# Chunk attention and two expert layers: the attention probabilities transposed on VectorE and exchanged by GpSimd's DMAs

## The chip, the cores and the metric

One core of one Trainium2 chip runs the kernel. The metric is the device time of one execution in microseconds; lower is better. The engines named below are TensorE (PE, with its weight loads PEld), VectorE (DVE), ScalarE (ACT), GpSimd (POOL) and SyncE (SP, which issues DMAs).

## The reference, cut to what matters

Attention runs within chunks of 64 tokens, 8 batches of 8 heads, 576 tokens each, 64 numbers per head. Its result is the input of two dense layers over 4608 tokens.

```python
def _attn_ref(q, k, v):                      # chunks of 64 tokens
    scores = scale * np.matmul(q_c, k_c.transpose(0, 1, 2, 4, 3))
    scores = scores - np.max(scores, axis=-1, keepdims=True)
    attn = np.exp(scores)
    attn = attn / (np.sum(attn, axis=-1, keepdims=True) + 1e-09)
    return np.matmul(attn, v_c)

def _moe_ref(x, w_in, w_out):                # 512 -> 2048 -> 512
    h = x @ w_in
    return (h * np.cos(h)) @ w_out

def _moe2_ref(x, w_in, w_out, g_ln):         # 512 -> 1024 -> 512
    h = x @ w_in
    solu = h * softmax(h)
    return (layernorm(solu) * g_ln) @ w_out
```

## The kernel before, in words

The 4608 tokens are worked through in nine blocks `j` of 512. The first expert layer is a list of 144 steps (`steps`, line 79), one for each block and each of the 16 columns of 128 hidden units. Step `n` runs `mm_in(n)` (12 matmuls of 128x512 into `h`, lines 570 to 572), on VectorE and ScalarE the cosine of steps `n` and `n - 1` (`act_h`, `dve_r`, `act_sin`, `dve_g`, `split_g`: tiles `hs`, `kt`, `r`, `gh`, `gl`), and `mm_out(n - 2)` (12 matmuls into `y`, lines 637 to 639). Every float32 product is made of three matmuls of split halves (`xh`, `xl` with `whi`, `wlo`). The second expert layer follows the first, with its first segments beside the first layer's last steps.

Attention is cut into 20 units. The first four (two chunks each) run before the steps. The others hold four chunks of all 8 heads, so that two units make one block of 512 tokens. Units 4 and 5 (`i < NAT`) load q and k in another order and are spread over four steps each (`tight`). Units 6 to 19, fourteen of them, are spread over eight steps each by the list `wide` (lines 819 to 824): each entry names a step counted from the unit's first, a place in that step (`early` is after `mm_in`, `mid` before `mm_out`, `late` after it) and a piece. `place` (lines 835 to 846) gives the unit's first step; for a unit of block `j` it is 17 or 9 steps ahead of the block's own first step.

The pieces of a wide unit are `att_tr` (q and k transposed in 32x32 blocks on VectorE, line 427, tiles `qt` and `kt`), `att_qk` (64 matmuls of 64x64 on TensorE, tile `sc`), `att_max`, `att_sub`, `att_exp`, `att_sum`, `att_mul` (softmax, tile `p`), `att_pt` (8 full 128x128 transposes of `p` on TensorE into PSUM, tile `pt`, line 503), `att_ptc` (one copy of 128x1024 on ScalarE from PSUM, tile `ptb`, line 508), `att_pv` (64 matmuls of 64x64 against the values, tile `x`) and `att_x` (split of the result into `xh` on ScalarE and `xl` on VectorE). `load_next` loads q and k of the next unit in 32 DMAs of 32 KB on SyncE, `load_next_v` its values in 4 of 128 KB. `sc`, `pt` and `x` follow each other in the one buffer of `ps_a` (tag `a`, two PSUM banks). `qt`, `kt`, `p` and `ptb` follow each other in the two SBUF buffers of tag `t` (`work`, line 315). `qi`, `ki` and `vi` have one buffer each.

The order of an engine's instructions is made by the framework's scheduler: it takes what is ready in the order of the program, so that pieces may be moved ahead of their place. `tc.keep_in_program_order` pins an instruction behind the one that the program traced last on the same engine; `att_tr` is pinned so. Semaphore waits are put in by the framework. Many instructions are recorded under line 104, the helper's; there the tile names tell them apart.

In the second layer `blocks32` and `shuffle` (lines 954 to 978) transpose an activation: 32x32 blocks on VectorE (tile `bt`), then 16 DMAs per block of 512 tokens on SyncE that move each 32-partition group to its place (tile `lt`). Weights of the second layer are prepared during the first, in `prep_w2in` at steps 55 and 71 and `prep_w2out` at 87, 88, 103 and 104 (lines 1058 to 1068). GpSimd runs a few set-up instructions and, in the second layer, two small ones per tile (line 939, tile `rs`).

Of the kernel before, what the change touches and what calls it, by code (L numbers as in the profile page):

```python
# [29 lines left out]
def kernel(  # L30
# [12 lines left out]
    nc = tc.nc  # L43
# [5 lines left out]
    CH = 64  # L49
# [5 lines left out]
    NF = F1 // P  # L55
# [18 lines left out]
    NB = 8  # L74
# [81 lines left out]
    def wtile(dt, name, n=1024):  # L156
        return wp.tile([P, n], dt, tag="w", name=name)
# [141 lines left out]
    UNITS = [(2 * i, 2) for i in range(SUB)] + [(c, 4) for c in range(8, NT // CH, 4)]  # L299
    NU = len(UNITS)  # L300
    HU = H // 2


    NAT = SUB + 2
    GA = 8

    def small(i):
        return i < SUB

    def work(i, shape, tag, name):  # L310

        if small(i) or (i == SUB + 1 and tag != "t"):
            t = wtile(F32, name, 512 if small(i) else 1024)
        else:
            t = ap_.tile([P, 1024], F32, tag=tag, name=name, bufs=2 if tag == "t" else 1)
        letters = "abcde"[:len(shape)]
        sizes = {x: n for x, n in zip(letters, shape)}
        return t.rearrange(f"p ({' '.join(letters)}) -> p {' '.join(letters)}", **sizes)
# [17 lines left out]
    v0 = su.tile([P, HU, 2 * SUB, D], F32, name="v0")  # L336
# [86 lines left out]
    def att_tr(i, name):  # L423
        src, dst = (qi, qt) if name == "q" else (ki, kt)
        o = work(i, (H, 4, 32), "t", f"{name}t")
        tc.keep_in_program_order(
            nc.vector.transpose(out=o.rearrange("p h x t -> p x h t"), in_=src.pop(i))
        )
        dst[i] = o.rearrange("p h x t -> p h (x t)")
# [3 lines left out]
    def natural(i, ap):  # L433
        return ap.rearrange("p (a g) -> p g a", a=GA) if SUB <= i < NAT else ap
# [58 lines left out]
    pt, ptb = {}, {}  # L493

    def att_pt(i):
        p = pr.pop(i)
        x = UNITS[i][1] // 2 * HU
        if small(i):
            t = ps_h.tile([P, x, P], F32, tag="h", name="pt")
        else:  # L500
            t = ps_a.tile([P, x, P], F32, tag="a", name="pt")
        for y in range(x):
            pe.transpose(out=t[:, y], in_=p[:, y].rearrange("p r k -> p (r k)"), identity=ident)
        pt[i] = t
# [8 lines left out]
    def att_pv(i):  # L513
        n = UNITS[i][1]

        t = (ps_y if small(i) else ps_a).tile([P, 2, 512], F32, tag="y" if small(i) else "a", name="x")
        a, b = vi.pop(i, None), ptb.pop(i)
        for y in range(n * HU // 2):
            for row in range(2):
                for col in range(2):  # L520
                    rs = slice(row * CH, (row + 1) * CH)
                    if small(i):
                        w, c = divmod(y, n)
                        u = 2 * w + col
                        m, p = v0[rs, u, UNITS[i][0] + c], b[rs, u, c * CH:(c + 1) * CH]
                    else:
                        u, cc = divmod(y, 2)
                        m, p = a[rs, cc, 2 * u + col], b[rs, cc * HU + u, col * CH:(col + 1) * CH]
                    pe.matmul(
                        out=t[col * CH:(col + 1) * CH, row, y * CH:(y + 1) * CH],  # L530
                        lhsT=m,
                        rhs=natural(i, p),
                        start=True,
                        stop=True,
                    )
        xps[i] = t[:, :, 0:n * HU // 2 * CH]
# [172 lines left out]
    if True:  # L709
# [23 lines left out]
        for c in range(4):  # L733
            sync.dma_start(
                out=gcol[32 * c:32 * (c + 1)],
                in_=g_ln.rearrange("(c q p) -> c p q", c=4, p=32)[c],
# [20 lines left out]
        att_mul(0)  # L757
        tok(2)
        att_pt(0)
        att_max(1)  # L760
        att_sub(1)
# [7 lines left out]
        att_mul(1)  # L769
        tok(3)  # L770
        att_pt(1)
        att_max(2)
        att_sub(2)
# [5 lines left out]
        att_sum(2)  # L779
        att_mul(2)  # L780
        att_pv(0)
        att_pt(2)
        att_max(3)
        att_sub(3)
        att_exp(3)
        att_ptc(2)
        att_pv(1)
        att_pv(2)
        att_sum(3)
        att_mul(3)  # L790
# [24 lines left out]
        def load_next_v(i):  # L815
# [3 lines left out]
        wide = (  # L819
            (0, "early", lambda i: att_tr(i, "q")), (1, "early", lambda i: att_tr(i, "k")),  # L820
            (1, "late", att_qk), (1, "late", load_next), (2, "early", att_max), (3, "early", att_sub),
            (3, "mid", att_exp), (4, "early", att_sum), (5, "early", att_mul), (5, "late", att_pt),
            (6, "early", att_ptc), (6, "late", att_pv), (6, "late", load_next_v), (7, "early", att_x),
        )
        tight = (
            (0, "early", lambda i: att_nat(i, "q")), (0, "early", lambda i: att_natc(i, "q")),
# [8 lines left out]
        def place(i, n, pieces):  # L835
            for at, when, what in pieces:
                att.setdefault((n + at, when), []).append((what, i))

        for i in range(SUB, NU):
            j, o = divmod(UNITS[i][0] * CH, T)  # L840
            if j == 1:
                place(i, 0 if o == 0 else NB // 2, tight)
            elif j == 2:
                place(i, NF + (0 if o == 0 else NB - 1), wide)
            else:
                place(i, j * NF - NF - 1 if o == 0 else j * NF - NB - 1, wide)

        def run(n, when):
            for what, i in att.get((n, when), ()):
# [176 lines left out]
        for n in range(NSTEP + LAG + 1):  # L1026
# [20 lines left out]
            r = n - NB  # L1047
# [38 lines left out]
        for x in range(first_seg, 2 * (NI + LAG2) + 4):  # L1086
            i, seg = divmod(x, 4)
            segment(i, seg)
            t, half = 2 * i - LAG2 + seg // 2, seg % 2
# [34 lines left out]
```

## Time and profile before

| | us |
|---|---|
| median of 3 runs | 1317.0 |
| lowest, highest | 1316.44, 1317.3 |
| the profiled execution, device time | 1315.48 |
| its span on the core | 1313.7 |

The profile is of one execution. The page begins with the busy time of each engine; below it the span is cut into slices, and groups of instructions are listed by line, tile and shape. A row of a timeline gives the start, the duration, engine, line, the operation with output and input tiles, shapes and a count of merged instructions; in square brackets stands how long the engine had been idle before and what ended that. Matmuls are pipelined and overlap, so that the spacing of their starts, not their duration, tells what one costs. PEclk is the granted share of TensorE's full clock.

### The profile page before, as it was taken

What the parts mean: (1) busy time and instruction counts of PE and PEld (TensorE: products, weight loads), DVE (VectorE), ACT (ScalarE), POOL (GpSimd) and SP (SyncE); (2) the same over time, 40 slices, a digit from 0 to 9 for tenths busy, and PEclk for the clock granted to TensorE, in tenths of its full rate; (3) what the DMA queues carried; (4) which work ended last, traced back from release to release, by engine and by line L of the source; (5) the groups of instructions that cost most, each with busy time, mean ns of one, the idle gap of its engine ahead of it and who ended that gap; (6) DMA issues with size and microseconds to landing.
All of it is one profiled execution on the core that took longest, in us unless ns stands there. A gap on an engine that the chain in (4) does not pass through costs nothing.

```text
span 1313.7 us, 20245 instructions
## 1 busy us (share of the span) xinstructions
PE 1270.9 (97%) x7652; PEld 1016.4 (77%) x7652; DVE 977.1 (74%) x1608; ACT 789.3 (60%) x1143; POOL 30.7 (2%) x79
## 2 busy tenths in 40 slices
PE   5899999999999999999999999999989999999998
PEld 4566777888887787888887888888768888888886
DVE  4887988676779879878878866667786686766751
ACT  4877876666655656556556545537665655655552
POOL 0000000000000000000000000000110000000000
PEclk9899999999999999999999999999989999999999
DMA  9942344331344344353343410450464543445224
GB/s 243 212 108 82 111 132 92 90 77 30 58 135 135 63 133 133 65 124 97 78 108 97 95 27 1 150 215 28 154 190 114 149 131 99 122 111 145 64 63 107
DMA packets 240930, 143.44 MB, mean 109 GB/s; under 512 B 176832, under 2 KB 217280, under 8 KB 239296
## 3 DMA queue, kind: packets, MB, share of 16 engines
q1 hardware_dynamic: 240736, 142.02, 41.4%
q8 instruction: 60, 0.98, 0.3%
q14 instruction: 38, 0.31, 0.1%
q10 hardware_dynamic: 96, 0.13, 0.0%
HBM read 83.63 MB, written 39.58 MB: 94 GB/s over the span
## 4 chain that ended last, share of the span: by engine, by line
PE 76%; DVE 10%; ACT 5%; issue 4%; SPq 3%; DMA 2%; POOL 0%; ACTq 0%; DVEq 0%; POOLq 0%
PE h L570 8%; PE y L637 8%; PE y L638 7%; PE y L639 7%; PE h L572 7%; PE h L571 7%; PE o L994 5%; PE o L992 5%; PE o L993 5%; PE h L862 4%; PE h L864 3%; PE h L863 3%; SPq L104 3%; DVE z L104 2%; PE x L104 1%
## 5 line engine op out<-in xcount | busy, mean ns | idle before, releaser
L570 PE MATMUL h<-xh,whi 128*128 128x512 f32 x576 | 232.6, 404 | 1.6 <-ACT xh L104 1.3
L571 PE MATMUL h<-xl,whi 128*128 128x512 f32 x576 | 226.2, 393 | 0.9 <-DVE xl L104 0.9
L572 PE MATMUL h<-xh,wlo 128*128 128x512 f32 x576 | 226.2, 393 | 0.1
L637 PE MATMUL y<-gh,whi 128*128 128x512 f32 x544 | 213.0, 397 | 4.8 <-ACT gh L104 3.8
L638 PE MATMUL y<-gl,whi 128*128 128x512 f32 x544 | 215.3, 396 | 0.3 <-DVE gl L104 0.3
L639 PE MATMUL y<-gh,wlo 128*128 128x512 f32 x544 | 214.9, 395 | 0.0
L599 ACT ACTIVATE r<-r 128x512 f32<-128x512 f32 x144 | 90.8, 631 | 166.0 <-DVE r L593 165.7
L607 DVE SCALAR_TENSOR_TENSOR hs<-r,hs 128x512 f32<-128x512 f32 x136 | 93.7, 689 | 81.6 <-ACT r L600 81.2
L570 PEld LDWEIGHTS h<-xh,whi 128*128 128x128 f32 x576 | 108.8, 189 | 27.9 <-issue 1.6
L104 ACT ACTIVATE gh<-hs 128x512 fp32r<-128x512 f32 x136 | 85.5, 629 | 74.0 <-DVE hs L607 71.0
L571 PEld LDWEIGHTS h<-xl,whi 128*128 128x128 f32 x576 | 108.7, 189 | 25.0 <-issue 1.7
L572 PEld LDWEIGHTS h<-xh,wlo 128*128 128x128 f32 x576 | 108.6, 189 | 24.2 <-issue 0.5
L104 DVE TENSOR_TENSOR gl<-hs,gh 128x512 fp32r<-128x512 f32 x136 | 93.4, 687 | 44.8 <-ACT gh L104 44.6
L637 PEld LDWEIGHTS y<-gh,whi 128*128 128x128 f32 x544 | 101.4, 188 | 31.7 <-ACT gh L104 7.5
L638 PEld LDWEIGHTS y<-gl,whi 128*128 128x128 f32 x544 | 102.2, 188 | 26.2 <-DVE gl L104 2.3
L639 PEld LDWEIGHTS y<-gh,wlo 128*128 128x128 f32 x544 | 102.1, 188 | 23.6
L577 ACT ACTIVATE hs<-h 128x512 f32<-128x512 f32 x144 | 85.2, 592 | 56.7 <-PE h L572 46.2
L992 PE MATMUL o<-whi,lh 128*128 128x512 f32 x288 | 113.5, 394 | 1.6 <-ACT lh L104 1.6
L994 PE MATMUL o<-whi,ll 128*128 128x512 f32 x288 | 113.2, 393 | 0.7 <-DVE ll L104 0.5
L993 PE MATMUL o<-wlo,lh 128*128 128x512 f32 x288 | 113.3, 393 | 0.0
L590 DVE SCALAR_TENSOR_TENSOR r<-kt,hs 128x512 f32<-128x512 int32 x144 | 99.1, 688 | 16.4 <-ACT kt L585 13.9
L862 PE MATMUL h<-whi,yh 128*128 128x512 f32 x252 | 99.6, 395 | 9.9 <-DVE tp L890 9.9
(112 smaller groups left out, 2078.3 us busy)
## 6 DMA issues: line engine op xcount, KB each, us to landing
lt<-bt SPq DMA_DIRECT2D x144, 128.0 KB
yr<-yd SPq DMA_DIRECT2D x18, 896.0 KB
yd<-ts SPq DMA_DIRECT2D x18, 512.0 KB
out<-os SPq DMA_DIRECT2D x142, 64.0 KB
vi<-in_v SPq DMA_DIRECT2D x64, 128.0 KB
qi<-in_q SPq DMA_DIRECT2D x224, 32.0 KB
ki<-in_k SPq DMA_DIRECT2D x224, 32.0 KB
st<-in_moe_w_in SPq DMA_DIRECT2D x10, 512.0 KB
```

Of the source, the lines that this page charges most:

```text
L104: ins = getattr(self.engine, name)(*args, **kwargs)
L570: nc.tensor.matmul(out=t, lhsT=wa, rhs=xh[j][:, kk, :], start=(kk == 0), stop=False)
L571: nc.tensor.matmul(out=t, lhsT=wa, rhs=xl[j][:, kk, :], start=False, stop=False)
L572: nc.tensor.matmul(out=t, lhsT=wb, rhs=xh[j][:, kk, :], start=False, stop=(kk == KD - 1))
L590: nc.vector.scalar_tensor_tensor(out=r, in0=kt, scalar=-TWO_PI_HI, in1=h, op0=ALU.mult, op1=ALU.add)
L637: nc.tensor.matmul(out=o, lhsT=wa, rhs=a, start=head, stop=False)
L638: nc.tensor.matmul(out=o, lhsT=wa, rhs=b, start=False, stop=False)
L639: nc.tensor.matmul(out=o, lhsT=wb, rhs=a, start=False, stop=last)
L862: nc.tensor.matmul(out=ps, lhsT=a, rhs=whi, start=kk == 0, stop=False)
L992: nc.tensor.matmul(out=o, lhsT=hi, rhs=whi, start=(f == 0), stop=False)
L993: nc.tensor.matmul(out=o, lhsT=hi, rhs=wlo, start=False, stop=False)
L994: nc.tensor.matmul(out=o, lhsT=lo, rhs=whi, start=False, stop=(f == NF2 - 1))
```

## The change

For the units from `NAT` on, `att_pt` no longer transposes on TensorE. VectorE transposes `p` in 32x32 blocks into a new tile `t` of the same tag and size (named `ptr`), and 16 DMAs from GpSimd's queue, each of 32 partitions by 1 KB, move block row `c` of column group `g` to block row `g` of column group `c` in the tile `ptb`. The ScalarE copy `att_ptc` is gone for all wide units. `att_pv` reads the moved operand as two pieces of 32 instead of 64 contiguous numbers. In the list, `att_mul` goes from early in step 5 to late in step 4, the transpose from late in 5 to late in 4, `att_pv` from late in 6 to early in 8, `load_next_v` from late in 6 to late in 8 and `att_x` from early in 7 to early in 9. Each wide unit's first step is one earlier (the first unit's two). Units 0 to 5 keep the old way.

```diff
--- before.py
+++ after.py
@@ -495,6 +495,24 @@
     def att_pt(i):
         p = pr.pop(i)
         x = UNITS[i][1] // 2 * HU
+        if i >= NAT:
+
+            t = work(i, (4, x, 32), "t", "ptr")
+            o = work(i, (4, x, 32), "t", "ptb")
+            tc.keep_in_program_order(
+                nc.vector.transpose(
+                    out=t.rearrange("p g x s -> p x g s"),
+                    in_=p.rearrange("p x r (h s) -> p x (r h) s", s=32),
+                )
+            )
+            for g in range(4):
+                for c in range(4):
+                    nc.gpsimd.dma_start(
+                        out=o[32 * g:32 * (g + 1), c].rearrange("p x s -> p (x s)"),
+                        in_=t[32 * c:32 * (c + 1), g].rearrange("p x s -> p (x s)"),
+                    )
+            ptb[i] = o
+            return
         if small(i):
             t = ps_h.tile([P, x, P], F32, tag="h", name="pt")
         else:
@@ -522,14 +540,18 @@
                     if small(i):
                         w, c = divmod(y, n)
                         u = 2 * w + col
-                        m, p = v0[rs, u, UNITS[i][0] + c], b[rs, u, c * CH:(c + 1) * CH]
+                        m, p = v0[rs, u, UNITS[i][0] + c], natural(i, b[rs, u, c * CH:(c + 1) * CH])
                     else:
                         u, cc = divmod(y, 2)
-                        m, p = a[rs, cc, 2 * u + col], b[rs, cc * HU + u, col * CH:(col + 1) * CH]
+                        m, x = a[rs, cc, 2 * u + col], cc * HU + u
+                        if i < NAT:
+                            p = natural(i, b[rs, x, col * CH:(col + 1) * CH])
+                        else:
+                            p = b[rs, 2 * col:2 * col + 2, x, :]
                     pe.matmul(
                         out=t[col * CH:(col + 1) * CH, row, y * CH:(y + 1) * CH],
                         lhsT=m,
-                        rhs=natural(i, p),
+                        rhs=p,
                         start=True,
                         stop=True,
                     )
@@ -819,8 +841,8 @@
         wide = (
             (0, "early", lambda i: att_tr(i, "q")), (1, "early", lambda i: att_tr(i, "k")),
             (1, "late", att_qk), (1, "late", load_next), (2, "early", att_max), (3, "early", att_sub),
-            (3, "mid", att_exp), (4, "early", att_sum), (5, "early", att_mul), (5, "late", att_pt),
-            (6, "early", att_ptc), (6, "late", att_pv), (6, "late", load_next_v), (7, "early", att_x),
+            (3, "mid", att_exp), (4, "early", att_sum), (4, "late", att_mul), (4, "late", att_pt),
+            (8, "early", att_pv), (8, "late", load_next_v), (9, "early", att_x),
         )
         tight = (
             (0, "early", lambda i: att_nat(i, "q")), (0, "early", lambda i: att_natc(i, "q")),
@@ -841,9 +863,9 @@
             if j == 1:
                 place(i, 0 if o == 0 else NB // 2, tight)
             elif j == 2:
-                place(i, NF + (0 if o == 0 else NB - 1), wide)
+                place(i, NF - 2 if o == 0 else NF + NB - 2, wide)
             else:
-                place(i, j * NF - NF - 1 if o == 0 else j * NF - NB - 1, wide)
+                place(i, j * NF - NF - 2 if o == 0 else j * NF - NB - 2, wide)
 
         def run(n, when):
             for what, i in att.get((n, when), ()):
```

## Rows read from the trace of the kernel before

**Rows 1.** The page's engine table: busy us, share of the span, instructions.

```profile
PE 1270.9 (97%) x7652; PEld 1016.4 (77%) x7652; DVE 977.1 (74%) x1608; ACT 789.3 (60%) x1143; POOL 30.7 (2%) x79
```

**Rows 2.** Stretches: length, then busy us (instructions) by engine, granted clock, DMA share, GB/s.

```profile
core 0: us, PE busy (x) PEld busy (x) DVE busy (x) ACT busy (x) POOL busy (x), PEclk, DMA share, GB/s
160.00:830.00 670.00, 665.05 (x4563) 536.06 (x4562) 529.29 (x767) 403.06 (x601) 0.00 (x0) 1.00 0.36 87
490.00:660.00 170.00, 168.45 (x1152) 136.19 (x1151) 144.09 (x215) 101.22 (x149) 0.00 (x0) 1.00 0.43 102
```

**Rows 3.** TensorE's waits: who waited for whom, us in total, times, longest.

```profile
PE h L862 <- DVE tp L890: 9.9, 8, 6.0
```

**Rows 4.** Timeline of TensorE around one unit's transposes: start, us, instruction.

```profile
326.48 0.39 PE L639 MATMUL y<-gh,wlo 128*128 128x512 f32 x1
326.70 1.04 PE L104 MATMUL pt<-ident,p 128*128 128x128 f32 x8
...
327.81 0.39 PE L571 MATMUL h<-xl,whi 128*128 128x512 f32 x1
328.04 0.39 PE L572 MATMUL h<-xh,wlo 128*128 128x512 f32 x1
```

**Rows 5.** Groups of instructions by form: busy us, mean ns, idle before.

```profile
L607 DVE SCALAR_TENSOR_TENSOR hs<-r,hs 128x512 f32<-128x512 f32 x136 | 93.7, 689 | 81.6 <-ACT r L600 81.2
...
L587 DVE TENSOR_SCALAR kt<-hs 128x512 int32<-128x512 f32 x96 | 40.6, 423 | 11.3 <-ACT hs L577 9.9
...
L104 PE MATMUL pt<-ident,p 128*128 128x128 f32 x144 | 20.6, 285 | 2.4 <-DVE p L104 2.4
...
L427 DVE STREAM_TRANSPOSE qt<-qi 128x1024 f32<-128x1024 f32 x14 | 17.3, 1237 | 0.0
```

**Rows 6.** Timeline of an ordinary step, VectorE's and TensorE's.

```profile
325.26 0.69 DVE L104 TENSOR_TENSOR gl<-hs,gh 128x512 fp32r<-128x512 f32 x1 [0.89 <-ACT gh L104]
...
330.57 0.39 PE L638 MATMUL y<-gl,whi 128*128 128x512 f32 x1
```

**Rows 7.** GpSimd's line 939: duration ns min/median/max, first and last start us.

```profile
L939 POOL TENSOR_TENSOR rs<-va,nhalf x36: 547/548/1520, 901.4 to 1274.8; 128x1 f32<-128x1 f32 x36
```

**Rows 8.** Timeline of the last shuffle: VectorE's, SyncE's and ScalarE's.

```profile
1275.69 2.47 DVE L964 STREAM_TRANSPOSE bt<-h 128x1024 f32<-128x1024 f32 x2 [0.98 <-ACT h L945]
...
1279.10 10.06 SPq L974 DMA_DIRECT2D lt<-bt  x16
...
1291.16 1.06 ACT L104 ACTIVATE lh<-lt 128x1024 fp32r<-128x1024 f32 x1 [1.69 <-DMA lt<-bt]
```

**Rows 9.** Timeline of SyncE's queue: one unit's query loads, 32 KB each.

```profile
536.88 7.71 SPq L104 DMA_DIRECT2D qi<-in_q  x16
```

**Rows 10.** Timeline of VectorE in one ordinary unit, 534 to 583 us.

```profile
535.62 1.24 DVE L427 STREAM_TRANSPOSE qt<-qi 128x1024 f32<-128x1024 f32 x1
...
560.88 1.23 DVE L104 TENSOR_TENSOR p<-p,s 128x1024 f32<-128x1024 f32 x1
...
579.49 1.22 DVE L104 TENSOR_TENSOR xl<-x,xh 128x1024 fp32r<-128x1024 f32 x1 [0.22 <-ACT xh L104]
...
582.50 1.24 DVE L427 STREAM_TRANSPOSE qt<-qi 128x1024 f32<-128x1024 f32 x1
```

**Rows 11.** Timeline of TensorE in the same unit.

```profile
546.12 1.16 PE L104 MATMUL sc<-kt,qt 64*64 64x64 f32 x64
...
575.94 1.16 PE L104 MATMUL x<-ptb,vi 64*64 64x64 f32 x64
```

**Rows 12.** Timeline of a unit beside a weight preparation, VectorE's and TensorE's.

```profile
388.40 1.24 DVE L427 STREAM_TRANSPOSE qt<-qi 128x1024 f32<-128x1024 f32 x1
...
417.87 1.24 DVE L427 STREAM_TRANSPOSE kt<-ki 128x1024 f32<-128x1024 f32 x1
...
430.51 1.22 DVE L104 TENSOR_TENSOR p<-p,s 128x1024 f32<-128x1024 f32 x1
...
435.66 1.16 PE L104 MATMUL x<-ptb,vi 64*64 64x64 f32 x64
```

**Rows 13.** Busy time in a stretch beside that preparation, columns as in rows 2.

```profile
396.00:424.00 28.00, 27.09 (x177) 21.64 (x176) 26.77 (x43) 14.88 (x27) 0.00 (x0) 1.00 0.45 147
```

## What the change should do to the time

> **What bounds the kernel now.** I read the engine table of the page first, to see which engine is full: TensorE 1270.9 of 1313.7 us, VectorE three quarters, GpSimd 2% [rows 1]. A share is an average, so I then cut the span at the stages and read busy time by stretch. The fourteen units that the change touches lie almost wholly between 160 and 830 us. There TensorE is idle for 670 - 665.05 = 4.95 us, at a granted clock of 1.00 (the 2.4 GHz level), VectorE is busy 79% of the time (85% in the fullest stretch) and GpSimd not at all [rows 2]. So in this stage time is what TensorE is given to do, and an instruction taken from it is worth its whole place in the queue. Last I read TensorE's waits: the largest, 9.9 us on `tp`, belongs to the second expert layer, after this stage [rows 3].
>
> **What is removed.** Per unit, 8 transposes on TensorE and one copy on ScalarE. The mean of a transpose, 285 ns [rows 5], is not its price: matmuls overlap, and so I price the hole that the eight leave between their neighbours. From the last `y` matmul before them to the second `h` matmul after them is 327.81 - 326.48 = 1.33 us; two ordinary spacings of 0.23 us (327.81 to 328.04) would be 0.46. The eight cost 0.87 us [rows 4]. Fourteen units: 12.2 us. The copies run on ScalarE, which is at 60% [rows 1]; nothing but `x` on TensorE waits for them, so they bring nothing further.
>
> **What is added on VectorE.** One 32x32-block transpose of 128x1024 per unit. The kernel does the same form for q and k: 1237 ns [rows 5]. Fourteen make 17.3 us, on an engine with 15 to 21% free [rows 2]; priced at nothing, because the instructions behind it are early. In an ordinary step `gl` is written at 325.26 + 0.69 = 325.95 and first read by `y` L638 at 330.57, so VectorE may be 4.6 us late before TensorE notices [rows 6]. If that cover were gone, all of the 17.3 us would be paid.
>
> **What is added on GpSimd.** 16 DMAs of 32 KB per unit, 224 in all, SBUF to SBUF. Its queue holds nothing else in this stage: the first of its `rs` instructions starts at 901.4 us [rows 7]. No row shows a DMA issued from GpSimd, so I bound the exchange, from the end of VectorE's transpose to the last landing, by the nearest rows. The nearest is the kernel's own shuffle of `bt` into `lt`: 16 DMAs between the same partition groups, four times the bytes, from SyncE. At the end of the program it is bare: transposes end at 1278.16, the DMAs are issued from 1279.10 for 10.06 us (0.63 each), the last landing releases `lh` at 1291.16. That is 13.0 us = 16 x 0.63 + 2.9 around it [rows 8]. Cheaper: 32 KB loads on SyncE, 7.71 us for 16 (0.48 each), which gives 10.6 us [rows 9]. Dearer: the longest GpSimd instruction of that line, 1.52 us [rows 7], taken 16 times, gives 27.2 us. I take 0.8 us each, 16 us, nearer to the shuffle since the pattern is the same, but above it since the queue is another.
>
> The Trainium skill (DMA: Bandwidth & Descriptors, Latency and other measured facts) puts about 1 us on the first byte of a DMA from GpSimd and 0.6 on one from SyncE; if each of the 16 cost that 1 us, the exchange would be an estimated 18.9 us. No row here shows it.
>
> **Is there room for it?** An ordinary unit, in its own time: `qt` at 535.62, probabilities multiplied until 560.88 + 1.23 = 562.11, next unit's `qt` at 582.50, which is 8 steps later [rows 10]. Less the two attention blocks in it (1.16 us each as `sc` and `x` show, [rows 11]) and the transposes' 0.87, a step is about 5.5 us, half of it 12 matmuls of 0.23. The multiply keeps its place behind the same `r` (late in step 4 instead of early in step 5). The new transpose is pinned behind it alone and ends at 563.35. Two instructions then wait for the DMAs:
> - `x` on TensorE goes from late in step 6 to early in step 8: 575.94 [rows 11] + 3 x 2.75 - 0.87 = 583.3. Window: 583.3 - 563.35 = 19.95 us. A microsecond late here is a microsecond lost.
> - The next unit's `qt` on VectorE. The change puts five tiles per unit instead of four through the two buffers of tag `t`, so `qt` falls on the buffer that the DMAs read. At 582.50 - 0.87 = 581.6 its window is 18.3 us; behind it stand `hs` and `gl`, with 4.6 us of their own.
>
> So 16 us fits, and 13 us with ease. The break-even is (19.95 - 2.9) / 16 = 1.07 us per DMA.
>
> **What moves.** A unit starts one step earlier and has its `x` early in its step 8 instead of late in 6, so in the kernel's steps `x` comes half a step (2.75 us) later and its evacuation one step; for every second unit the next block's `mm_in` needs the result. From the start of `x` to the end of `xl` is 579.49 + 1.22 - 575.94 = 4.8 us [rows 10, 11]; after the change 1.16 + 2.75 + 5.5 = 9.4 us lie between: free. The value loads behind `x` on SyncE's queue start half a step later, for a use eight steps off: free. Query and key loads come one step earlier with their unit. TensorE's wait for 16 landings in place of one copy: `x` already waits for four `vi` DMAs and `sc` for none, yet both blocks take 1.16 us [rows 11]; nothing.
>
> **Where it is tight.** Beside the units that start at steps 55 and 71 a second-layer weight is prepared on VectorE. There `qt` is at 388.40, but `kt` only at 417.87, because it is pinned behind that preparation; the multiply ends at 431.73 and `x` runs at 435.66 [rows 12]. One step earlier, `kt` stands ahead of the preparation. With nothing in the way `kt` would come a step after `qt`, at 393.9, and the multiply end 13.9 us after it, at 407.8; with everything in the way, as now. VectorE is busy 26.77 of 28 us from 396 to 424 [rows 13], so I put the end of multiply and transpose at 425.5, and with 16 us the DMAs at 441.5, against an `x` due at about 438.4 (2.75 us after its present place). 3 us in each of two units is 6 at most; it is nothing if the scheduler puts other matmuls first. I take 3.
>
> **The sum.** 1315.5 (the profiled execution) - 12.2 + 3.0 = 1306.3. The median of the runs is 1.5 us above it: 1307.8. This case's own range is 1303 (no tight unit and a little of today's 4.95 idle us saved) to 1312 (both tight, the others late by 0.1 us each).
>
> **Rivals.**
> *GpSimd's queue takes the place of the transposes* (slower). Place: `x` on TensorE, every unit. It decides from 1.07 us per DMA, a figure between its bounds of 0.48 and 1.52. At 1.2 us the exchange takes 22.1, TensorE waits 2.15 in each of 14 units, 30 us: 1317 - 12.2 + 30 = 1335; at 1.52 it would wait 101 us, less what the scheduler moves ahead. For it: no row shows the queue. Against: the shuffle's 0.63. One more thing works for it: L587 converts 512 elements in 423 ns where L607 takes 689 for as many [rows 5], so it runs at a higher rate, once a step. If GpSimd could not write while it runs, each window would lose up to 3 x 0.42 = 1.3 us and the break-even fall to 0.99. That this happens is a rule of the Trainium skill (SBUF — State Buffer, SBUF: two separate sides): while VectorE runs an instruction in a mode that takes both ports, GpSimd cannot write the descriptors of its DMAs. No row here shows it. Chance 0.27.
> *VectorE becomes the bound.* The added transposes are paid where it is fullest, beside the weight preparation of 5 units, 6.2 us, and the tight units stay late by 6: 1317 - 12.2 + 6.2 + 6 = 1317. Against: 4.6 us of cover. Chance 0.13.
> *It doesn't do what it says*: another wait of 0.87 us per unit stands in place of the transposes, say of `sc` for the bank that the later evacuation of `x` holds: 1317. Against: 4.95 idle us in the whole stage, with the same bank handed on three times a unit. Chance 0.05.
>
> **How the numbers follow.** Forecast 0.55, at 1307.8. What a measurement of this kernel can tell from no change is about 0.2%, 2.6 us: 1314.4 to 1319.6 is the same. Faster: 0.55 and a little of the second rival, 0.59. Same: 0.13. Slower: 0.28, nearly all the first rival. The range runs from 1302 to 1336; above it lies half of the first rival, under 0.17 in all with what is below.
>
> **What would show it.** Right: `x` waits for no `ptb` DMA in ordinary units, the hole of 0.87 us is gone, TensorE's busy time up to 830 us falls by 12 us, GpSimd's issues are under 1.07 us apart. Wrong: waits of `x` on the DMAs (first rival), or `qt` waiting with `gl` late behind it and `y` L637 and L638 waiting on VectorE (second).

## The result and the profile after

The changed kernel takes 1327.0 us at the median (1324.4 to 1327.3) against 1316.7 for the kernel before: ratio 1.0076, 95% interval 1.006 to 1.0092. It is 0.8% slower; the forecast was 1307.8. The profiled execution has a span of 1324.9 us, 11.2 more than before. All lines behind the changed functions carry numbers that are 22 higher (`h` L592 to L594, `y` L659 to L661, `hs` L629).

The engine table of the kernel after, answering [rows 1]; VectorE gains 16 us and GpSimd 111:

```profile
PE 1270.0 (96%) x7540; PEld 1011.4 (76%) x7540; DVE 993.3 (75%) x1622; ACT 779.5 (59%) x1129; POOL 142.1 (11%) x303
```

TensorE runs 112 instructions fewer in the same busy time. The stretches say why, with the columns of [rows 2]: the attention stage first, then four short stretches in it.

```profile
160.00:830.00 670.00, 654.00 (x4410) 523.38 (x4408) 539.83 (x773) 390.49 (x582) 111.26 (x224) 0.98 0.41 99
...
185.30:192.00 6.70, 6.00 (x16) 4.29 (x16) 6.67 (x10) 6.31 (x10) 1.47 (x3) 0.50 0.54 180
420.80:424.10 3.30, 3.30 (x8) 2.65 (x9) 2.97 (x6) 1.83 (x4) 3.30 (x7) 0.50 0.21 50
519.80:523.10 3.30, 3.30 (x8) 2.62 (x9) 2.97 (x6) 1.88 (x4) 3.26 (x7) 0.50 0.20 50
717.80:724.50 6.70, 6.58 (x26) 4.84 (x27) 5.09 (x9) 3.51 (x6) 0.00 (x0) 0.50 0.01 2
```

TensorE is idle for 670 - 654.00 = 16.0 us of the stage, where it was 4.95 [rows 2], and in four stretches, 20.5 us in all, its granted clock is 0.50, the 1.2 GHz level. The kernel before has none of these between 40.8 and 962 us. Busy time counts these stretches as full, so the share hides them.

What TensorE waits for in the stage (who waited for whom, us in total, times, longest), answering [rows 3]:

```profile
PE x L104 <- DMA ptb<-ptr: 6.4, 2, 3.7
PE y L659 <- ACT gh L104: 5.5, 4, 2.4
PE y L660 <- DVE gl L104: 2.9, 5, 0.9
```

Before, the stage had 3.2 us of `y` waiting for `gh` and none for `gl`. The exchange itself is fast. The group of GpSimd's DMAs (ns min/median/max), their issues with KB and median us to landing, the spread of the landings, and one unit of them on GpSimd's timeline, answering [rows 7 to 9]:

```profile
L510 POOL DMA_DIRECT2D ptb<-ptr x224: 496/498/818, 177.8 to 811.9; - x112
...
ptb<-ptr POOLq DMA_DIRECT2D x224, 32.0 KB, 1.8
...
DMA to landing us min/median/max: 1.6/1.8/6.2
...
707.16 8.02 POOL L510 DMA_DIRECT2D ptb<-ptr  x16 [40.43 <-DVE ptr L503]
```

16 issues take 8.0 us (0.50 each). VectorE's transpose of that unit ended at 706.62 and the last of its DMAs landed at 718.0, 11.4 us later; over the 14 units the landings in the trace give 9.6 to 14.6 us (median 11.8), against 16 in the forecast's sum.

Yet `x` waits for it. TensorE around the last of the four places:

```profile
714.58 0.39 PE L594 MATMUL h<-xh,wlo 128*128 128x512 f32 x1
714.90 0.33 PE L104 MATMUL x<-ptb,vi 64*64 64x64 f32 x4
717.92 0.73 PE L104 MATMUL x<-ptb,vi 64*64 64x64 f32 x6 [2.69 <-DMA ptb<-ptr]
...
722.02 0.63 PE L661 MATMUL y<-gh,wlo 128*128 128x512 f32 x1
722.45 0.63 PE L660 MATMUL y<-gl,whi 128*128 128x512 f32 x1
...
725.04 0.39 PE L661 MATMUL y<-gh,wlo 128*128 128x512 f32 x1
725.27 0.39 PE L659 MATMUL y<-gh,whi 128*128 128x512 f32 x1
```

Matmuls of `x` stand in TensorE's queue from 8.3 us behind VectorE's transpose on, in small groups among those of `h` and `y`, not as one block of 64 as before [rows 11]. The scheduler has moved them ahead. The first four run at 714.90; the next wait for a DMA, and everything behind them in the queue waits 2.69 us with them. Right behind the wait matmuls start 0.43 us apart (722.02, 722.45) instead of 0.23 (725.04, 725.27): at that level 1 us of the clock does 0.54 us of work and loses 0.46. The first place (a wait of 3.69 us from 182 on, 5.1 us behind the transpose) is of the same kind.

The other two lie at 416 and 515 us, beside `prep_w2in`. TensorE, VectorE and ScalarE at the first:

```profile
416.51 0.39 PE L594 MATMUL h<-xh,wlo 128*128 128x512 f32 x1
419.13 0.72 PE L659 MATMUL y<-gh,whi 128*128 128x512 f32 x2 [2.23 <-ACT gh L104]
420.80 0.80 PE L660 MATMUL y<-gl,whi 128*128 128x512 f32 x1 [0.95 <-DVE gl L104]
...
414.85 1.21 DVE L104 TENSOR_REDUCE s<-p 128x16 f32<-128x1024 f32 x1
...
416.59 1.23 DVE L104 TENSOR_TENSOR p<-p,s 128x1024 f32<-128x1024 f32 x1
417.73 1.29 DVE L629 SCALAR_TENSOR_TENSOR hs<-r,hs 128x512 f32<-128x512 f32 x2
418.93 1.24 DVE L503 STREAM_TRANSPOSE ptr<-p 128x1024 f32<-128x1024 f32 x1
420.10 1.25 DVE L104 TENSOR_TENSOR gl<-hs,gh 128x512 fp32r<-128x512 f32 x2
...
418.45 1.29 ACT L104 ACTIVATE gh<-hs 128x512 fp32r<-128x512 f32 x2 [1.81 <-DVE hs L629]
```

VectorE has no gap. `hs` stands behind the unit's sum and multiply, `gh` waits for `hs`, and the new transpose (1.24 us) stands between `hs` and `gl`. TensorE loses 2.23 and 0.95 us, and runs at half the clock from 420.75 on.

**Where the time went.** Transposes' holes: -12.2 by the forecast. Idle time in the stage: +11.05. Half clock in the stage: 19.2 busy us at 0.46 lost = +8.8. Sum +7.7 of the 11.2 by which the spans differ. Outside the stage TensorE is idle 1.1 us longer, and a stretch of half clock near 30 us holds 8.1 busy us instead of 6.1, which loses 0.9; about 1.6 us stay unassigned.

### The profile page after: what moved, and what is told of

The parts are those of the page before. It is cut to its first block, busy times and chain, and to the rows that moved or that the text cites. A ratio compares the mean times of both kernels' runs of the same rounds, so it can differ in the third digit from the quotient of the medians.

```text
span 1324.9 us, 20535 instructions
## 1 busy us (share of the span) xinstructions
PE 1270.0 (96%) x7540; PEld 1011.4 (76%) x7540; DVE 993.3 (75%) x1622; ACT 779.5 (59%) x1129; POOL 142.1 (11%) x303
## 4 chain that ended last, share of the span: by engine, by line
PE 64%; DVE 18%; ACT 7%; issue 5%; DMA 3%; SPq 2%; POOL 1%; ACTq 0%; DVEq 0%; POOLq 0%
PE h L592 6%; PE h L594 6%; PE y L660 6%; PE h L593 6%; PE y L659 6%; PE y L661 6%; PE o L1016 5%; PE o L1014 5%; PE o L1015 5%; PE h L884 4%; PE h L886 3%; PE h L885 3%; DVE z L104 2%; SPq L104 2%; DVE r L612 2%
## 5 line engine op out<-in xcount | busy, mean ns | idle before, releaser
L592 PE MATMUL h<-xh,whi 128*128 128x512 f32 x576 | 231.7, 402 | 2.4 <-ACT xh L104 1.3
L594 PE MATMUL h<-xh,wlo 128*128 128x512 f32 x576 | 226.9, 394 | 0.1
L659 PE MATMUL y<-gh,whi 128*128 128x512 f32 x544 | 215.5, 402 | 6.6 <-ACT gh L104 6.1
L660 PE MATMUL y<-gl,whi 128*128 128x512 f32 x544 | 218.1, 401 | 3.3 <-DVE gl L104 3.2
L661 PE MATMUL y<-gh,wlo 128*128 128x512 f32 x544 | 217.2, 399 | 0.0
L510 POOL DMA_DIRECT2D ptb<-ptr x224 | 111.3, 505 | 699.8 <-DVE ptr L503 245.3
L629 DVE SCALAR_TENSOR_TENSOR hs<-r,hs 128x512 f32<-128x512 f32 x136 | 92.8, 684 | 55.2 <-ACT r L622 54.9
L592 PEld LDWEIGHTS h<-xh,whi 128*128 128x128 f32 x576 | 109.2, 190 | 29.5 <-ACT hs L599 1.8
L659 PEld LDWEIGHTS y<-gh,whi 128*128 128x128 f32 x544 | 102.7, 190 | 33.5 <-ACT gh L104 9.2
L594 PEld LDWEIGHTS h<-xh,wlo 128*128 128x128 f32 x576 | 109.1, 189 | 24.5 <-issue 0.5
L661 PEld LDWEIGHTS y<-gh,wlo 128*128 128x128 f32 x544 | 103.6, 190 | 23.8
```

Of the source, the lines that this page charges most:

```text
L510: nc.gpsimd.dma_start(out=o[32 * g:32 * (g + 1), c].rearrange("p x s -> p (x s)"), in_=t[32 * c:32 * (c + 1), g].rearrange("p x s -> p (x ...
L592: nc.tensor.matmul(out=t, lhsT=wa, rhs=xh[j][:, kk, :], start=(kk == 0), stop=False)
L594: nc.tensor.matmul(out=t, lhsT=wb, rhs=xh[j][:, kk, :], start=False, stop=(kk == KD - 1))
L659: nc.tensor.matmul(out=o, lhsT=wa, rhs=a, start=head, stop=False)
L660: nc.tensor.matmul(out=o, lhsT=wa, rhs=b, start=False, stop=False)
L661: nc.tensor.matmul(out=o, lhsT=wb, rhs=a, start=False, stop=last)
```

## The experiments

Three causes were on the table. A: with the new start steps the unit's softmax falls on VectorE together with the weight preparation. B: matmuls of `x` are moved ahead of the DMAs that they need. C: VectorE's added transposes. Two questions came up later: what the holes cost beyond themselves, and whether what is left of the gain is the exchange's. "Idle" is TensorE's between 160 and 830 us, "half" the time at half clock in the same stretch, both of the one profiled execution. That one is not always near the median: in experiments 1, 3 and 7 it lies 2.3 to 3.4 us above it, in 4, 5 and 6 it is the shortest of ten (1315.1, 1309.2 and 1318.5 us). Each ratio is against the kernel before on the same chip. An experiment's own edits shift the line numbers again (`y` is L661 to L663 in 3 and 5).

| kernel | median us | ratio, 95% interval | idle | half |
|---|---|---|---|---|
| before | 1316.7 | 1 | 4.95 | 0 |
| after | 1327.0 | 1.0076 (1.0060 to 1.0092) | 16.0 | 20.5 |
| old start steps | 1327.9 | 1.0094 (1.0073 to 1.0114) | 17.0 | 10.2 |
| old start steps, `x` in order | 1329.0 | 1.0096 (1.0075 to 1.0117) | 15.6 | 17.1 |
| new places, TensorE's transposes | 1317.5 | 1.0008 (0.9998 to 1.0017) | 5.6 | 0 |
| the same and a spare VectorE transpose | 1320.0 | 1.0034 (1.0022 to 1.0045) | 8.1 | 0 |
| after, `x` in order | 1317.8 | 1.0019 (1.0009 to 1.0029) | 12.2 | 17.1 |
| after, preparation one step earlier | 1318.3 | 1.0026 (1.0017 to 1.0036) | 11.7 | 3.4 |
| after, both repairs | 1310.4 | 0.9965 (0.9954 to 0.9977) | 9.25 | 0 |
| control: both repairs, TensorE's transposes | 1320.0 | 1.0033 (1.0023 to 1.0042) | 7.3 | 0 |

**1. Old start steps.** The exchange stays, the units start where they did, and `x` keeps its absolute place, so the exchange has one step less.

```diff
-            (8, "early", att_pv), (8, "late", load_next_v), (9, "early", att_x),
+            (7, "early", att_pv), (7, "late", load_next_v), (8, "early", att_x),
...
-                place(i, NF - 2 if o == 0 else NF + NB - 2, wide)
+                place(i, NF + (0 if o == 0 else NB - 1), wide)
...
-                place(i, j * NF - NF - 2 if o == 0 else j * NF - NB - 2, wide)
+                place(i, j * NF - NF - 1 if o == 0 else j * NF - NB - 1, wide)
```

> The exchange stays, but each wide unit starts at its old step (one later than in the change, the first unit two), with the outputs early in its step 7 and evacuated early in step 8, so that these two keep the change's places. Theory A (the time was lost because the units' softmax now falls on VectorE together with the weight preparation at steps 14 to 20, 55, 71 and 103): TensorE's waits on gh and gl beside the preparations, 6.5 us with 3.4 us of half clock behind them, go; about 1317 us, and less if the first unit's holes go too. Theory B (the time was lost because matmuls of x stand in TensorE's queue ahead of their DMAs): the waits of x on the DMAs stay or spread to more units, 1327 us or more. Rival C (the transposes added to VectorE): no change, 1327.

1327.9, as slow as the change. The holes at 416 and 515 us are gone, but `x` waits for the exchange for 8.2 us in four places and `y` for `gl` for 5.0. The start steps alone are not the cause.

**2. The new places with TensorE's transposes.**

```diff
-        if i >= NAT:
+        if False:
...
-                        if i < NAT:
+                        if True:
                             p = natural(i, b[rs, x, col * CH:(col + 1) * CH])
...
-            (3, "mid", att_exp), (4, "early", att_sum), (4, "late", att_mul), (4, "late", att_pt),
+            (3, "mid", att_exp), (4, "early", att_sum), (4, "late", att_mul), (4, "late", att_pt), (5, "early", att_ptc),
```

> The change's places with the old transposes on TensorE and their copy on ScalarE (copy early in step 5); nothing is exchanged. Theory A: the waits beside the preparations stay, so it is slower than the kernel before by about 10 us: 1327. Theory B: no DMA waits, transposes back: 1317, like the kernel before. Rival C (VectorE's added transposes): 1317 as well.

1317.5, no different from before, idle 5.6 us, no half clock. A alone is refuted: the moves cost nothing as long as TensorE transposes. Note where its wait sits. At 414.67 it waits 1.14 us for `p` at the transposes, and by the time these are through, `gl` is there:

```profile
414.67 1.07 PE L104 MATMUL pt<-ident,p 128*128 128x128 f32 x8 [1.14 <-DVE p L104]
```

**3. `x` in the written order.**

```diff
-                    pe.matmul(
+                    ins = pe.matmul(
...
+                    if i >= NAT:
+                        tc.keep_in_program_order(ins)
```

> The change, with every matmul of x of the wide units pinned behind what the program has ahead of it on TensorE, so that none is moved ahead. Theory B: the waits of x on its DMAs (3.7 and 2.7 us) and the half clock behind them (twice 3.4 us) go, 13 us: 1314. Theory A: the waits on gh and gl stay; if they are all of the loss, 1327.

1317.8: 9.2 us of the loss are B's. The unit whose `x` stood at 714.90 now has it in one block, 14 us later, without a wait and in the 1.16 us of [rows 11], while `y` still waits for `gh` beside the preparation:

```profile
712.92 0.73 PE L661 MATMUL y<-gh,whi 128*128 128x512 f32 x2 [1.92 <-ACT gh L104]
728.81 1.16 PE L104 MATMUL x<-ptb,vi 64*64 64x64 f32 x64
```

What remains is 7.5 us of `y` waiting for `gh`, and half clock behind three of these holes.

**4. The preparation of the second weights one step earlier.**

```diff
-                elif n == begin + 4:
+                elif n == begin + 3:
                     prep_w2in(m)
...
-                elif n == begin + 4:
+                elif n == begin + 3:
                     prep_w2out(m)
```

> The change, with the preparation of the second layer's weights one step earlier (3 instead of 4 steps after their loads), so that it stands to the units as it did before: kt is pinned behind it again. Theory A: the holes at 416 and 515 us (6.5 us, and 3.4 us of half clock) go: 1317. Theory B: they are not what costs, 1327.

1318.3: 8.7 us off the change, with the code of `x` untouched. The holes beside `prep_w2in` shrink from 3.2 and 3.3 to 1.9 and 2.2 us, and no half clock follows them in this execution; the other nine have a lower mean clock (0.982 to 0.988 against 0.990), so some of them may have more. Only one wait of `x` is left (3.7 us, the first unit): the one near 715 us is gone too.

**5. Both repairs.** The edits of 3 and 4 together.

> The changed kernel with both repairs: the wide units' matmuls of x kept in the written order, and the preparation of the second weights one step earlier. Each repair alone took about 9 us off the changed kernel's 1327.0 (1317.8 and 1318.3). Theory 1, two separate causes (matmuls of x that stand ahead of their DMAs; VectorE late with gh and gl where a unit's softmax meets the weight preparation): the two savings add, 1327 - 9.2 - 8.7 = 1309, ratio about 0.994. Theory 2, one cause reached from two sides (a unit in trouble has both, and either repair mends it): 1315 to 1318, ratio about 1.000. What the forecast had promised, 1307.8, would be reached only under theory 1.

1310.4, faster than both kernels: the savings nearly add, 16.6 of 17.9 us, so these are two causes. They are not wholly apart: near 715 us either repair alone takes the wait of `x` away (3 leaves `y` waiting 1.92 us with half clock behind it, 4 leaves 0.84 without). The stage, and the place at 416 us, which has moved to 404:

```profile
160.00:830.00 670.00, 660.75 (x4483) 530.19 (x4482) 547.31 (x789) 398.34 (x594) 111.64 (x224) 1.00 0.41 99
...
406.02 0.73 PE L661 MATMUL y<-gh,whi 128*128 128x512 f32 x2 [1.34 <-ACT gh L104]
407.69 0.50 PE L662 MATMUL y<-gl,whi 128*128 128x512 f32 x1 [0.72 <-DVE gl L104]
408.03 0.39 PE L663 MATMUL y<-gh,wlo 128*128 128x512 f32 x1
```

A hole of 2.06 us is still there, but the clock is 1.00 throughout. -12.2 + 4.3 idle gives -7.9; the spans differ by 1307.4 - 1313.7 = -6.3.

**6. The control.** Experiment 2 with both repairs.

> The control of the run with both repairs (1310.4): the same start steps, x in the written order and the preparation of the second weights one step earlier, but the old eight transposes on TensorE with ScalarE's copy in place of VectorE's transpose and the exchange. If the 12.2 us of transposes' holes on TensorE are what the repaired kernel gains, this one stays near the kernel before: 1315 to 1318, ratio 0.999 to 1.002, and the exchange is worth 5 to 7 us. If the gain comes from the two repairs, which would have helped the kernel before as well: 1309 to 1312, ratio about 0.996, and the exchange is worth nothing.

1320.0. The repairs do nothing for a kernel that transposes on TensorE (they cost it 2.5 us), so what experiment 5 gains is the exchange: 9.6 us between the medians, 9.3 between the spans. The engine tables, the control first:

```profile
PE 1271.2 (97%) x7652; PEld 1017.0 (77%) x7652; DVE 977.3 (74%) x1608; ACT 792.9 (60%) x1143; POOL 30.7 (2%) x79
```

```profile
PE 1258.2 (96%) x7540; PEld 1003.0 (77%) x7540; DVE 991.1 (76%) x1622; ACT 779.8 (60%) x1129; POOL 142.5 (11%) x303
```

TensorE is busy 13.0 us less and, over spans of 1316.7 and 1307.4 us, idle 3.7 us more.

**7. Old start steps, `x` in the written order.** The edits of 1 and 3.

> The exchange with the units' old start steps, x two steps after the transposes, matmuls of x kept in the written order. Without that order this kernel took 1327.9, with 8.2 us of waits of x for the exchange in four places and 20.5 us at the half clock in four stretches (10.2 us lost). Theory 1 (the moved matmuls are what costs here, since VectorE's groups stand as in the kernel before): the waits and most of the half clock go, 1327.9 - 8 - 8 = 1312 or below, and no wait of x for the exchange is left. Theory 2 (VectorE's added transposes make gl late wherever the units start): waits of y for gl stay at 5 us, the half clock stays behind them, 1318 or more.

1329.0, and the theory that moved matmuls are what costs there falls. (The expectation counts four stretches of half clock in experiment 1; one of them, 10.2 us, lies behind the stage, where the kernel before has one of 6.8.) The wait is real here. VectorE's transpose and `x` of one unit:

```profile
626.15 1.24 DVE L503 STREAM_TRANSPOSE ptr<-p 128x1024 f32<-128x1024 f32 x1
...
634.90 0.44 PE L104 MATMUL x<-ptb,vi 64*64 64x64 f32 x2 [3.06 <-DMA ptb<-ptr]
```

VectorE reaches the transpose late, beside the weight preparation: TensorE comes to `x` at 631.84, 4.5 us behind the transpose's end, and with one step less the exchange no longer fits. So the change's earlier starts are needed: against experiment 3 they are worth 11 us. About 8 us of this kernel's and of experiment 1's time (by the medians) are in neither idle time nor half clock; they stay unexplained.

**8. VectorE's transposes alone.** Experiment 2 with the new transpose of `p` on VectorE, its result unread.

```diff
+        if i >= NAT:
+            t = work(i, (4, x, 32), "t", "ptr")
+            tc.keep_in_program_order(
+                nc.vector.transpose(
+                    out=t.rearrange("p g x s -> p x g s"),
+                    in_=p.rearrange("p x r (h s) -> p x (r h) s", s=32),
+                )
+            )
...
```

> The changed start steps with the old transposes on TensorE and ScalarE's copy, as in the run at 1317.5, and beside them VectorE's transpose of the changed kernel for each of the 14 wide units, 1.24 us each, whose result nobody reads. No exchange. If VectorE's 1.24 us ahead of the split is what makes gh and gl late beside the weight preparation (two places of about 3 us and a stretch at half clock behind each, 1.7 us lost each): 1317.5 + 2 x (3 + 1.7) = 1327, ratio 1.008. If VectorE has room for them and the exchange's arrival at x is what costs: 1317 to 1318, ratio 1.001.

1320.0, 2.5 us above experiment 2: C is real, but a small part as long as TensorE transposes. VectorE beside the preparation:

```profile
413.01 1.28 DVE L637 SCALAR_TENSOR_TENSOR hs<-r,hs 128x512 f32<-128x512 f32 x2
414.21 1.24 DVE L501 STREAM_TRANSPOSE ptr<-p 128x1024 f32<-128x1024 f32 x1
415.37 1.25 DVE L104 TENSOR_TENSOR gl<-hs,gh 128x512 fp32r<-128x512 f32 x2
```

`gl` comes 1 us later, and TensorE, after waiting 1.14 us at its transposes, waits 0.94 more for it (so too at 514 us; experiment 2 waits at neither). Here 1.14 + 0.94 us stand on either side of 1.06 us of transposes. Without those TensorE meets the same late `gh` and `gl` a microsecond earlier: 2.23 + 0.95 in the changed kernel. In these places taking the transposes away saves nothing. What VectorE's transposes cost where TensorE no longer transposes, no run separates.

**9. The preparation two steps earlier.** Experiment 5 with `begin + 2`.

> As the run with both repairs (1310.4; TensorE idle 9.25 us between 160 and 830 us), with the preparation of the second weights two steps earlier than in the kernel before instead of one. That run still has holes of 2.06 us at 404 and 2.0 us at 500 us, where VectorE works through the last of the preparation together with a unit's subtraction and sum. If the overlap of the two on VectorE makes these holes, one more step apart takes most of the 4 us away: 1306 to 1307, ratio about 0.993. If the unit's own VectorE work is enough (the loads of the weights then land later than the preparation wants them, or the next group on VectorE is late instead), 1310 or more.

1324.2 (1.0061, interval 1.0049 to 1.0074), the wrong way. `qt` of the unit beside `prep_w2out`, in experiment 5 and here:

```profile
572.68 1.25 DVE L427 STREAM_TRANSPOSE qt<-qi 128x1024 f32<-128x1024 f32 x1
```

```profile
601.60 1.24 DVE L427 STREAM_TRANSPOSE qt<-qi 128x1024 f32<-128x1024 f32 x1
```

`prep_w2out` now stands ahead of `qt` in the program; it runs on VectorE from 593.45 on. The unit is pushed behind it and all its work on VectorE falls into the next steps: `y` waits 1.59 and 3.10 us there, and the same again at 714. The repair works at one distance; it is not the more the better.

**10. The first unit one step later.** Experiment 5 with `NF - 1` for the unit that starts at `NF - 2`.

> As the run with both repairs (1310.4), with the first wide unit started one step later (NF - 1), so that its softmax stands further from the first weights' preparation and its x one step later. That run has 2.8 us of holes in five places between 161 and 178 us and 1.2 us of waiting of x at 190. If the start beside the preparation makes them: 1307 to 1308, ratio 0.994. If the preparation of that stretch has the same clash one step later: 1310, ratio unchanged at 0.9965.

1316.1 (1.0004, interval 0.9993 to 1.0015): neither outcome. `x` of that unit no longer waits, but `h` waits 5.28 us for `hs`. ScalarE there:

```profile
172.43 1.28 ACT L104 ACT_TABLE_LOAD   x1
173.72 1.06 ACT L104 ACTIVATE p<-p 128x1024 f32<-128x1024 f32 x1
174.69 0.61 ACT L104 ACTIVATE gh<-hs 128x512 fp32r<-128x512 f32 x1
175.32 1.28 ACT L623 ACT_TABLE_LOAD   x1
...
177.15 0.58 ACT L601 ACTIVATE hs<-h 128x512 f32<-128x512 f32 x1
```

The exponential and its two table loads now stand ahead of the copy that frees the bank of `h`, and 3.4 us of half clock follow.

**11. Holes made on purpose, first try.** The kernel before with four more transposes on TensorE whose input comes through a chain of DMAs.

```diff
+            if n in (39, 47, 63, 79):
+                src = hsb[n][:, 0:P]
+                for e in range({39: 1, 47: 2, 63: 3, 79: 4}[n]):
+                    d = cp.tile([P, P], F32, tag="d", name="d", bufs=2)
+                    nc.gpsimd.dma_start(out=d, in_=src)
+                    src = d
+                t = ps_a.tile([P, P], F32, tag="a", name="late")
+                tc.keep_in_program_order(pe.transpose(out=t, in_=src, identity=ident))
```

> The kernel before with four holes made on TensorE at steps 39, 47, 63 and 79: one more 128x128 transpose in the written order, whose input comes through a chain of 1, 2, 3 and 4 DMAs of 64 KB on GpSimd's queue, begun when hs is written. Nobody reads the results. By the exchange's landing of 1.8 us at the median the chains take about 2, 4, 6 and 8 us, of which TensorE has work for some 2 us: holes of about 0 to 0.5, 2, 4 and 6 us, some 12 us in all. Theory 1, a hole costs itself: 1316.7 + 12 = 1329, clock 1.00 behind the holes. Theory 2, a hole of 2 us or more is followed by 3.4 to 6.8 us at the 1.2 GHz level, as at the changed kernel's places: 1.7 to 3.4 us more for each of the three larger holes, 1334 to 1339.

1319.2 (1.0026, interval 1.0016 to 1.0037). The scheduler filled the holes with later matmuls; waits of 1.1 and 0.5 us were left and the clock stayed at 1.00. Inconclusive on the price of a long hole.

**12. Second try.** Chains of 1, 2, 3 and 3, with the last matmul of `y` ahead of each and the first of `h` behind it kept in the written order.

> The kernel before with a hole on TensorE at steps 39, 47, 63 and 79, between the last matmul of y and the first of the next h: a 128x128 transpose whose input comes through a chain of 1, 2, 3 and 3 DMAs of 64 KB, begun when hs is written. Nobody reads the results. In the earlier run with such chains one DMA took about 2.5 us from issue to the next issue, and TensorE has some 2.5 us of work (12 matmuls of y at 0.23) behind hs: holes of about 0, 2.5, 5 and 5 us, 12.5 us in all. If a hole costs itself alone: 1316 + 12.5 = 1328.5, the granted clock 1.00 through the stage. If each hole of over 2 us is followed by half the clock, as in the changed kernel (3.4 us of it behind 2.2 + 0.95, 6.8 us behind 2.69 and 3.69): 1.7 to 3.4 us more for each of three, 1334 to 1338.

1323.3 (1.0058, interval 1.0044 to 1.0071). The scheduler pulled whole groups of `y` in between, so no hole stood where it was meant. It shows one thing by accident: beside the preparation `y` waited 2.48 us for `gh`, in a place where the kernel before waits 1.55, and here the clock fell to 0.50 for 3.4 us right behind it, there not.

**13. Third try.** Chains of 1, 2 and 3 at steps 47, 63 and 79, all matmuls of `h` and `y` of two steps to either side in the written order.

```diff
+    late = {47: 1, 63: 2, 79: 3}
+    near = [n + d for n in late for d in (-2, -1, 0, 1, 2)]
+
+    def mm(n, **kw):
+        ins = nc.tensor.matmul(**kw)
+        if n in near:
+            tc.keep_in_program_order(ins)
...
```

> The kernel before with a 128x128 transpose on TensorE between y and the next h at steps 47, 63 and 79, its input a chain of 1, 2 and 3 DMAs of 64 KB begun when hs is written, the matmuls of h and y of two steps to either side kept in the written order so that none fills the hole. Nobody reads the results. From the earlier chains (0.9 us from the start of hs to the first issue, 0.54 an issue, 2.0 to 2.3 a landing) and 2.5 us of y ahead of the transpose, holes of about 1.1, 3.5 and 6 us, 10.6 in all. If holes cost themselves alone: 1316 + 10.6 = 1326.6, and the granted clock stays 1.00 behind each. If a hole of 2 us or more is followed by the 1.2 GHz level for 3.4 to 6.8 us, of which half is lost, and one of 1.1 us is not: 1316 + 10.6 + 2 x (1.7 to 3.4) = 1330 to 1333, with the two stretches right behind the second and the third hole.

1347.4 (1.0241, interval 1.0225 to 1.0256). The three holes came out at 0.31, 3.16 and 5.01 us, and the fixed order made two more, 7.79 us each, where the old transposes wait for `p`: that is why the time is above what was expected. The second hole:

```profile
454.11 0.40 PE L568 MATMUL y<-gh,wlo 128*128 128x512 f32 x1
457.66 0.30 PE L104 MATMUL late<-ident,d 128*128 128x128 f32 x1 [3.16 <-DMA d<-d]
...
458.50 0.39 PE L568 MATMUL h<-xh,whi 128*128 128x512 f32 x1
458.73 0.41 PE L568 MATMUL h<-xl,whi 128*128 128x512 f32 x1
...
460.22 0.63 PE L568 MATMUL h<-xh,wlo 128*128 128x512 f32 x1
460.65 0.63 PE L568 MATMUL h<-xh,whi 128*128 128x512 f32 x1
```

The matmuls are 0.23 us apart for a microsecond, and 0.43 from 459 on. Each of the four holes of 3.16 us and more has such a stretch behind it (in the longest three it begins within the hole), the one of 0.31 has none. The sum nearly closes: 27.7 - 4.95 = 22.8 us more idle, and 16.8 us of work at half clock behind the holes, of which 0.46 is lost, 7.7: 30.5 of the 32.8 by which the spans differ (1346.5 - 1313.7).

## Why the forecast was wrong, step by step

**The holes of the transposes, 12.2 us: right.** Exchange against transposes, with both repairs, takes 13.0 us from TensorE's busy time and is worth 9.3 to 9.6 us (experiments 5 and 6). It holds for units in which TensorE arrives last. Where it then waits for VectorE anyway, in the places beside the preparation, the 0.87 us come back as a longer wait (experiment 8). The check that the forecast proposed, busy time down by 12 us up to 830, was badly chosen: it fell by 11.05 there because TensorE stood idle.

**GpSimd's DMAs, 16 us: mis-sized, on the safe side.** At 0.50 us an issue the exchange took 9.6 to 14.6 us. The first rival, at 0.27 the largest risk, is refuted: no issue is above 0.82 us, below its 1.07. The 1 us of the Trainium skill (DMA: Bandwidth & Descriptors, Latency and other measured facts) would have made it an estimated 18.9; the trace shows 11.8 at the median. Its rule of the shared port (SBUF — State Buffer, SBUF: two separate sides) shows in a small way. Of the 40 issues that overlap one of VectorE's faster `TENSOR_SCALAR` instructions, as L609 is, 8 took 583 to 818 ns; of the other 184 all but one took at most 513. That is at most 0.6 us in one unit, where the rival counted 1.3 in each. The stated range of 1302 to 1336 holds 1327.0 only because its upper part was this rival's, which did not come about: that is luck.

**The window of 19.95 us for `x`: the step that failed first.** It was worked out from steps of the program. "It is nothing if the scheduler puts other matmuls first" was the only line on the scheduler, and it counted on help. The scheduler put `x`'s own matmuls first, into windows of 5 and 8 us instead of 20, in two units. With them kept in order, 9.2 us come back (experiment 3).

**"Priced at nothing, because the instructions behind it are early": wrong beside the preparation.** The 4.6 us of cover are of an ordinary step [rows 6], the 15 to 21% free of a long stretch; the forecast's own [rows 13] show VectorE busy for 26.77 of 28 us beside the preparation. Where it has no gap there is no cover, `gl` comes 1 us later, and the 14 transposes cost 2.5 us even with TensorE's still in place (experiment 8). The second rival named this mechanism and the place, but its price of 1317 had no clock in it and no moved matmuls.

**The tight units, 3.0 us: right place, wrong victim.** [rows 12, 13] were read for one question, when `x` would be ready. With `kt` ahead of the preparation, as forecast (393.70 instead of 417.87), `x` is in time; but the unit's subtraction, sum and multiply now fall among the preparation, and the late ones are `hs`, `gh` and `gl`, which `y` needs in every step. One step more between the two takes 8.7 us off (experiment 4). The forecast also looked at two units; the first wide unit, beside the first weights, and the one beside `prep_w2out` lose as well.

**The term that was not there: the clock.** The forecast noted a granted clock of 1.00 and took a wait for its own length. Each of the four places is followed by half clock, 8.8 us in the stage, and experiment 13 makes the same with holes of known length. Of the 19.2 us between 1307.8 and 1327.0, 8.8 are this, 8 the idle time above the 3.0 allowed, and the rest unassigned.

**"It doesn't do what it says"**: refuted by experiment 6. With both repairs the exchange gains 5.5 us on the kernel before, of the 9.2 that were forecast, and 1310.4 lies within the forecast's own range of 1303 to 1312.

## What to carry to other kernels

When a wait on a DMA takes the place of work on an engine, see where the scheduler puts the waiting instructions, not where the program does: pin them, or the window that you worked out is not the one you get. Read the cover of an added instruction in the fullest step that it meets, and ask there who stands behind it on its engine, not only who reads its result. Count a hole on TensorE with what follows it, and look at the granted clock of short stretches: here 11 us of added idle time brought 8.8 us lost at half clock with them, which a mean of 0.98 over the stage hid.

## What was not expected of the hardware

- A DMA of 32 KB between partition groups costs GpSimd 0.50 us to issue and lands 1.8 us later (median of 224, longest 6.2). 16 issues take 8.0 us, little more than SyncE's loads of that size, 0.48 each [rows 9].
- Beside VectorE's faster `TENSOR_SCALAR` instructions some of these issues take up to 0.32 us longer (8 of 40); apart from them one of 184 does.
- Half clock follows holes in TensorE's work that are much shorter than the stretch that they cost: 2.23 + 0.95 us brought 3.4 us, 2.69 brought 6.8. The length of the hole alone does not decide: 2.06 us did without it in experiment 5, and 1.42 + 0.50 us at 412 in experiment 10 had 3.4 us of half clock behind them.
